# A window-attention and gated-FFN kernel on one core: warm-up matmuls into another bank, full-width maxima, fewer f32 low halves, another order of the work

## The chip, the cores and the metric

One Trainium2 chip, one of its cores. The metric is the device time of one execution in microseconds (us). Besides the timed executions there is one that the hardware profiler took; its page and trace are what "the profile" means below. Engines: PE is TensorE, ACT is ScalarE, DVE is VectorE, POOL is GpSimd; SP only issues DMAs here.

## What is computed

Windowed attention, whose output goes as the activations into a gated feed-forward block:

```python
scores = scale * np.matmul(q, k.transpose(0, 1, 3, 2))      # (8, 8, 576, 576), head size 64
mask = (rel >= 0) & (rel < 64)                              # 64 keys back, causal
attn = softmax(np.where(mask, scores, -1e9))
x = matmul(attn, v).transpose(0, 2, 1, 3).reshape(4608, 512)
h = x @ w_in                                                # 512 -> 2048
sp = np.maximum(h, 0.0) + np.log1p(np.exp(-np.abs(h)))      # softplus
out = (h * erf(sp)) @ w_out                                 # 2048 -> 512
```

The two weight matrices reach the chip as 64-bit floats and are turned into numbers that PE can multiply on the chip itself.

## The kernel before, in words

**Precision.** Every operand of a large product is split into a high and a low half in f16, after scaling by a power of two; a product is the sum of three: high with high, high with low, low with high. The power of two comes from a maximum: of a chunk of q, k and v (`chunk_max`, `chunk_rows`, `chunk_top`, `chunk_all`, `chunk_scale`, L345 to L364), and of a pair of weight pieces (`bound`, `pair_rows`, `pair_top`, `pair_all`, `pair_scale`, L485 to L507). In both, DVE or ACT reduces along the free axis, a small matmul against the identity (L350; L495) lays the 128 partitions' values out in a row, DVE takes the maximum of the row, a second small matmul with a matrix of ones (L358; L501) spreads it over all partitions, and DVE reads it back (L361 into `cpw`; L304 into `kw`).

**Tiles.** 4608 tokens are 36 units of 128 and 18 chunks of 256. A unit's attention is 48 score matmuls of a 64x64 corner of the array (`scores`, L391), masked maximum, subtraction, two exponentials, transposes by DMA, and two times 24 matmuls of 128x64 weights (`weigh`, L424) into the PSUM tile `av`. The feed-forward block runs in 36 groups, a group being one chunk with one half of the 2048 hidden columns. A group is four blocks of 24 matmuls of 256 columns (`mm1`, L569) into one of the two banks `hp`; an eviction of each block by ACT or DVE (`hidden`, L312 or L314); softplus and erf on ACT (L581, L585), each with its own function table, whose loads show as ACT_TABLE_LOAD; a product on DVE (L589); a split into `gh` and `gl` (L312 or L314; L319); and twice 16 matmuls with `gh` and 8 with `gl` of 512 columns (`mm2`, L605) into the two banks `o`.

**Weights.** w_in and w_out come in 16 pieces of 1 MB (`fetch`). A piece is made into f32 by three passes of DVE and ACT (L475, L479, L483), bounded (L489 or L491), and scaled into its high half (`high`). Its low half is made in one of two ways. `low` is one DVE pass (L319). `low_sum` and `low_out` go by PE: an f32 matmul with a diagonal matrix (two passes, L532) and an f16 matmul that subtracts the high half (L533) into an `o` bank, twice for a piece, each followed by an eviction on ACT or DVE (L439 or L441). Before the change 11 pieces go by PE and 5 by DVE. Pieces 0 to 3 are needed before the first group, 4 to 7 before the second, 8 to 11 before the first `mm2`.

**Warm-ups.** `warm` issues matmuls of the identity with itself (L622) whose result nobody reads, at eight places between the start and the first `mm1`, 508 in all. They write `idle`, a stretch of the PSUM tile `av`; the small matmuls for the maxima write other stretches of the same tile (`crow`, `call`, `wrow`, `wall`).

**Order.** All of this is emitted from one list of tokens, `PLAN`, in a manual schedule: each engine runs its instructions in the list's order. A token names a handler, its indices and sometimes an engine (`a` ACT, `v` DVE, `g` POOL). In this text `wm:2:17` is 17 warm-ups, `pb` and `py` the two small matmuls of a chunk's maxima, `mb` and `my` those of a weight pair, `lp` one of a piece's two sums on PE, `s` and `a` a unit's scores and half of its weighing, `mm`, `mA` and `mB` the blocks of `mm1` and the `gh` and `gl` parts of `mm2`, `ev` an eviction of `hp`, `fo` an eviction of `o`. So the order on each engine, and the engine of each step that has a choice, are set by hand in the list.

```python
row_at = HP * (D + 1)
crow, call = avb[:3, 0, row_at:row_at + P], avb[:, 0, row_at + P:row_at + P + 3]
wrow, wall = avb[:1, 1, row_at:row_at + P], avb[:, 1, row_at + P:row_at + P + 1]
idle = avb[:, 0, row_at + P + 3:row_at + P + 123]
```

Of the kernel before, what the change touches and what calls it, by code (L numbers as in the profile page):

```python
# [213 lines left out]
def window_attention_gated_ffn(ctx, tc, q, k, v, w_in, w_out, masks, out):  # L214
# [27 lines left out]
    kwo = fixed("kwo", [P, 2])  # L242
    pm = fixed("pm", [P, 2])
    pr = fixed("pr", [P, 2])
    cmx, cpw, csc, cde = (cells(n, NCH, 3) for n in ("cmx", "cpw", "csc", "cde"))
    ctop, cdiag = fixed("ctop", [3, NCH]), fixed("cdiag", [3, NCH, 3], BF16)
    wtop = fixed("wtop", [1, 8], BF16)
    ident = fixed("ident", [P, P], BF16)
# [442 lines left out]
```

## Time and profile before

| | |
|---|---|
| median of 3 runs | 942.07 us (941.08 to 944.35) |
| the profiled execution | 943.69 us |
| its span, first to last instruction | 941.8 us |
| mean granted clock of PE | 0.982 |
| busy: PE, ACT, DVE, POOL | 906.7, 724.5, 701.2, 238.1 us |
| matmuls | 9282 |

A matmul's busy time includes the way through the array, which overlaps with the next one's; what a block of matmuls costs PE is read from its start to the start of what follows. PE runs its matmuls in the list's order, so such differences add up to the span without gaps or overlaps. Three stretches are told apart below: from the start to the first `mm1` block at 83.3 us, from there to the first `mm2` block of the second group at 185.2 us, by when the last weights have been made, and the rest.

### The profile page before, as it was taken

How to read it: one execution, taken by the hardware profiler on the slowest of the kernel's cores; microseconds unless marked ns; L12 is line 12 of the kernel's file. 1: busy time of each engine (PE TensorE's matmuls, PEld its weight loads, DVE VectorE, ACT ScalarE, POOL GpSimd, SP SyncE). 2: the span in 40 equal slices, each digit the busy share in tenths (PEclk: the TensorE clock that was granted, in tenths of full speed). 3: DMA queues.
4: the chain of work that ended last, by engine and by line, in shares of the span. 5: the costliest groups of instructions: out<-in, count | busy, mean ns of one | idle time of the engine just before them, and what ended most of it. 6: DMA issues, size and time to landing. Idle time of an engine off the chain costs nothing.

```text
span 941.8 us, 22242 instructions
## 1 busy us (share of the span) xinstructions
PE 906.7 (96%) x9282; PEld 606.3 (64%) x9282; DVE 701.2 (74%) x1533; ACT 724.5 (77%) x831; POOL 238.1 (25%) x231
## 2 busy tenths in 40 slices
PE   7778899999999999999999999999999999999998
PEld 6555657756656766666666766666767566676663
DVE  5567788888886877697887778888887776855542
ACT  5657899799974898889869798886969584966452
POOL 0022333320211122022232225341534260501000
PEclk8789899999999999999999999999999999999999
DMA  9655575542342445144543435444433424121000
GB/s 368 243 99 159 93 208 114 151 106 86 95 120 69 115 75 147 30 140 94 121 112 80 113 90 111 126 86 101 107 113 76 117 42 95 33 59 24 23 24 22
DMA packets 140533, 98.63 MB, mean 105 GB/s; under 512 B 117777, under 2 KB 117905, under 8 KB 140433
## 3 DMA queue, kind: packets, MB, share of 16 engines
q1 hardware_dynamic: 140432, 97.22, 40.7%
q8 instruction: 72, 1.18, 0.5%
q14 instruction: 29, 0.23, 0.1%
HBM read 59.44 MB, written 9.44 MB: 73 GB/s over the span
## 4 chain that ended last, share of the span: by engine, by line
PE 80%; ACT 7%; DVE 5%; DMA 5%; issue 1%; POOL 0%; SPq 0%; DVEq 0%; ACTq 0%
PE o L605 34%; PE hp L569 34%; PE av L424 3%; PE o L532 3%; PE av L622 3%; PE s L391 2%; DMA xt<-xs 2%; DMA vr<-v_in 1%; ACT y L581 1%; DMA stage<-w_out 1%; ACT L581 1%; ACT y L585 1%; ACT L585 1%; PE o L533 1%; DVE y L589 1%
## 5 line engine op out<-in xcount | busy, mean ns | idle before, releaser
L569 PE MATMUL hp<-xt,w 128*128 128x256 f16 x3456 | 397.3, 273 | 5.7 <-DMA xt<-xs 5.3
L569 PEld LDWEIGHTS <-w 128*128 128x128 f16 x3456 | 334.6, 98 | 63.8 <-issue 6.0
L605 PE MATMUL o<-w,gh 128*128 128x512 f16 x1152 | 260.7, 380 | 0.6 <-DVE ob L614 0.6
L605 PEld LDWEIGHTS <-gh 128*128 128x128 f16 x1152 | 110.4, 98 | 123.7 <-issue 1.4
L605 PE MATMUL o<-w,gl 128*128 128x512 f16 x576 | 136.5, 380 | 0.0
L405 POOL TENSOR_TENSOR sm<-sm,mx 128x512 f32<-128x512 f32 x56 | 69.4, 1244 | 204.0 <-DVE mx L400 203.9
L581 ACT ACTIVATE y<-h 128x1024 f32<-128x1024 f32 x72 | 75.8, 1056 | 53.4 <-DVE h L314 52.8
L589 DVE TENSOR_TENSOR y<-h,y 128x1024 f32<-128x1024 f32 x72 | 92.2, 1281 | 29.9 <-ACT y L585 29.7
L319 DVE SCALAR_TENSOR_TENSOR gl<-y,sg,gh 128x1024 f16<-128x1024 f32 x72 | 97.5, 1355 | 16.8 <-PE o L605 12.8
L314 DVE TENSOR_SCALAR h<-hp,c 128x512 f32<-128x512 f32 x95 | 70.8, 746 | 42.0 <-PE hp L569 41.4
L581 ACT ACT_TABLE_LOAD x68 | 87.2, 1283 | 7.9 <-DVE h L314 6.7
L605 PEld LDWEIGHTS <-gl 128*128 128x128 f16 x576 | 53.4, 98 | 55.3
L585 ACT ACT_TABLE_LOAD x67 | 86.0, 1283 | 1.2
L585 ACT ACTIVATE y<-y 128x1024 f32<-128x1024 f32 x72 | 75.9, 1056 | 0.8
L400 DVE CUSTOM_DVE_ANT_0 sm<-s,mask 128x128 f32<-128x128 f32 x288 | 65.1, 285 | 11.1 <-PE s L391 10.3
L414 POOL TENSOR_TENSOR p<-sm,p 128x512 f16<-128x512 f32 x36 | 47.8, 1329 | 93.1 <-ACT sm L410 93.0
L409 ACT ACTIVATE p<-sm,shift,cde 128x512 f16<-128x512 f32 x72 | 58.1, 807 | 15.4 <-POOL sm L405 12.1
L447 POOL TENSOR_TENSOR xs<-x,xs 128x512 f16<-128x512 f32 x26 | 36.3, 1397 | 96.9 <-ACT xs L439 59.4
L410 ACT ACTIVATE sm<-sm,shift,cde 128x512 f32<-128x512 f32 x72 | 58.6, 814 | 2.4
L319 DVE SCALAR_TENSOR_TENSOR vs<-vr,csc,vs 128x1024 f16<-128x1024 f32 x36 | 55.0, 1527 | 1.8 <-POOL vs L316 1.5
L312 ACT ACTIVATE gh<-y,sg 128x1024 f16<-128x1024 f32 x39 | 44.3, 1137 | 9.7 <-PE o L605 7.0
L312 ACT ACTIVATE h<-hp,c 128x512 f32<-128x512 f32 x49 | 33.1, 678 | 24.1 <-PE hp L569 24.1
(129 smaller groups left out, 980.3 us busy)
## 6 DMA issues: line engine op xcount, KB each, us to landing
vr<-v_in SPq DMA_DIRECT2D x36, 512.0 KB, 4.1
kr<-k_in SPq DMA_DIRECT2D x36, 384.0 KB, 3.6
qr<-q_in SPq DMA_DIRECT2D x36, 256.0 KB, 3.6
out<-ob SPq DMA_DIRECT2D x36, 256.0 KB, 2.1
stage<-w_out SPq DMA_DIRECT2D x6, 1024.0 KB, 5.0
stage<-w_in SPq DMA_DIRECT2D x4, 1024.0 KB, 7.0
w<-w_in SPq DMA_DIRECT2D x2, 1024.0 KB, 11.0
w<-w_out SPq DMA_DIRECT2D x2, 1024.0 KB, 4.9
```

What stands on the lines that cost most here:

```text
L312: nc.scalar.activation(dst, src, AF.Copy, scale=s)
L314: nc.vector.tensor_scalar(dst, src, s, None, op0=ALU.mult)
L319: nc.vector.scalar_tensor_tensor(dst, src, s, hi, op0=ALU.mult, op1=ALU.subtract)
L400: nc.vector.tensor_tensor_reduce(smi(u, par)[:, j, :], sps[par][:, j, :], mask[:, var, :], 1.0, LOWEST, op0=ALU.add, op1=ALU.max, accum_ou ...
L405: eng_of(eng).tensor_tensor(s, s, m.unsqueeze(2).broadcast_to([P, HP, P]), op=ALU.subtract)
L409: nc.scalar.activation(pp[0][u % 2][:, HP * par:HP * par + HP, :], s, AF.Exp, bias=shift14, scale=es)
L410: nc.scalar.activation(s, s, AF.Exp, bias=shift14, scale=es)
L569: nc.tensor.matmul(hps[pc % 2][:, f, :], w1[a][:, cc, fs], xt[b][c % 2][:, cc, :], start=(n == 0), stop=(n == 3 * NCC - 1))
L581: nc.scalar.activation(at(yb, g, n), at(hb, g, n), AF.Softplus)
L585: nc.scalar.activation(y, y, AF.Erf)
L589: nc.vector.tensor_tensor(y, at(hb, g, n), y, op=ALU.mult)
L605: nc.tensor.matmul(ops[j], a[:, f, ts], w2[b][:, hf * GF + f, :], start=f == 0 and a is gh and b == 0, stop=f == GF - 1 and a is gl)
```

## The change

Four things.

1. `idle` becomes a stretch of the bank `hp0`, and there are 334 warm-ups at seven places in place of 508 at eight.
2. The two small matmuls of a chunk's maxima are given the array's full size. The stationary operand of the first is 128x128 in place of 128x3 (`cmx` is one tile of 128 columns, of which three are used and the others are zero); that of the second is 128x128 ones in place of 3x128, with a moving operand of 128 partitions whose rows from the fourth on are zero. POOL gets two more memsets at the start. The small matmuls of the weight pairs stay as they are.
3. 7 pieces have their low halves made by PE, and 9 by DVE (`lp` and `le` 22 to 14 each, `l` 5 to 9). Of the `lp` tokens that are left out, one stood before the first `mm1` and seven stood between it and the second group's `mm2`; there two are left of nine.
4. `PLAN` is another list. What it computes is the same, and the engines of many steps differ: `ev` is on ACT 88 times and on DVE 56 times (49 and 95 before). A unit's two `a` tokens stand side by side more often, and next to an `s`: PE goes to such attention work and away from it 48 times in place of 86, and changes between `s` and `a` within one such visit 26 times in place of 7. ACT's list has 175 table loads in place of 171.

```diff
-    "L:1 L:0 lq:0 L:3 L:2 lk:0 L:5 lk:1 lq:1 lm wm:0:126 lv:1 lv:0 d:1 c:1 L:4 o:1 b:1:v c:0 d:0 pk:0:0:a o:0 b:0:a "
...
-    cmx, cpw, csc, cde = (cells(n, NCH, 3) for n in ("cmx", "cpw", "csc", "cde"))
-    ctop, cdiag = fixed("ctop", [3, NCH]), fixed("cdiag", [3, NCH, 3], BF16)
+    cpw, csc, cde = (cells(n, NCH, 3) for n in ("cpw", "csc", "cde"))
+    cmx = fixed("cmx", [P, P])
+    ctop, cdiag = fixed("ctop", [3, NCH]), fixed("cdiag", [P, NCH, 3], BF16)
...
-    ones = fixed("ones", [3, P], BF16)
+    ones = fixed("ones", [P, P], BF16)
...
-    crow, call = avb[:3, 0, row_at:row_at + P], avb[:, 0, row_at + P:row_at + P + 3]
+    crow, call = avb[:, 0, row_at:row_at + P], avb[:, 0, row_at + P:row_at + P + 3]
...
-    idle = avb[:, 0, row_at + P + 3:row_at + P + 123]
...
+    idle = hps[0][:, 0, :120]
...
+    nc.gpsimd.memset(cmx, 0.0)
+    nc.gpsimd.memset(cdiag, 0.0)
...
     def chunk_max(c):
-        nc.vector.tensor_reduce(cmx[c], peaks[:, :, c * TPC:(c + 1) * TPC + 1], axis=AX.X, op=ALU.max)
-        exponent(cmx[c], cmx[c])
+        top = cmx[:, :3]
+        nc.vector.tensor_reduce(top, peaks[:, :, c * TPC:(c + 1) * TPC + 1], axis=AX.X, op=ALU.max)
+        exponent(top, top)
 
     def chunk_rows(c):
-        nc.tensor.matmul(crow, powers(cmx[c]), ident, start=True, stop=True)
+        nc.tensor.matmul(crow, powers(cmx), ident, start=True, stop=True)
 
     def chunk_top(c):
         top = ctop[:, c:c + 1]
-        nc.vector.tensor_reduce(top, crow, axis=AX.X, op=ALU.max)
-        nc.vector.scalar_tensor_tensor(cdiag[:, c], top.broadcast_to([3, 3]), FLOOR, ident[:3, :3], op0=ALU.max, op1=ALU.mult)
+        nc.vector.tensor_reduce(top, crow[:3], axis=AX.X, op=ALU.max)
+        nc.vector.scalar_tensor_tensor(cdiag[:3, c], top.broadcast_to([3, 3]), FLOOR, ident[:3, :3], op0=ALU.max, op1=ALU.mult)
```

The lines of the changed kernel stand two higher than those of the kernel before in most of the code (L624 for L622).

**First place: PE in the start-up, at the second weight pair's `my`.** `wtop` is the pair's maximum, `ident` the warm-ups' operand, `diag` and `minus` the operands of a low half. Before:

```order
L533 MATMUL o_155<-w_0_137,minus 128x512
L501 LDWEIGHTS ones
L501 MATMUL av<-wtop,ones 128x1
L622 LDWEIGHTS ident
L622 MATMUL av<-ident 128x120
```

Now:

```order
L535 MATMUL o_156<-w_0_137,minus 128x512
L503 LDWEIGHTS ones
L503 MATMUL av<-wtop,ones 128x1
L352 LDWEIGHTS cmx
L352 MATMUL av<-ident,cmx 128x128
L360 LDWEIGHTS ones
L360 MATMUL av<-cdiag,ones 128x3
L534 MATMUL o_156<-w_0_139,diag_88 128x512
```

Where 52 warm-ups followed (`wm:3:52`), the two matmuls of the first chunk's maxima follow now, ahead of the third piece's sums; they stood behind the warm-ups and behind one of these sums each.

**Second place: PE in the steady part, at the end of unit 18's first `a` token.** `pt` and `vs` are operands of `a`, `qs` and `ks` of `s`. Before, the array goes from the 64-column weights of `a` back to `mm1`; the unit's second `a` token follows a block later:

```order
L424 LDWEIGHTS pt_0_124
L424 MATMUL av<-vs_0_115,pt_0_124 64x65
L424 LDWEIGHTS pt_0_126
L424 MATMUL av<-vs_0_113,pt_0_126 64x65
L569 LDWEIGHTS w_0_137
L569 MATMUL hp_154<-xt_0_133,w_0_137 128x256
```

Now the second `a` token follows at once, and at its end unit 20's scores follow:

```order
L426 LDWEIGHTS pt_0_124
L426 MATMUL av<-vs_0_115,pt_0_124 64x65
L426 LDWEIGHTS pt_0_126
L426 MATMUL av<-vs_0_113,pt_0_126 64x65
L393 LDWEIGHTS qs_0_105
L393 MATMUL s_150<-ks_0_109,qs_0_105 64x128
```

Two `a` tokens and an `s` make one visit, where they made three.

**Third place: ACT between the softplus of groups 13 and 14.** `h<-hp` is an eviction (`ev`), `y<-h` softplus, `y<-y` erf, `p` and `sm` exponentials of the attention, `gh` a high half. Before:

```order
L312 ACTIVATE gh<-y_144,sg 128x1024
L312 ACTIVATE h_141<-hp_153,c_89 128x512
L409 ACTIVATE p_1_121<-sm_118,shift_64,cde 128x512
L410 ACTIVATE sm_118<-sm_118,shift_64,cde 128x512
L312 ACTIVATE h_141<-hp_154,c_89 128x512
L581 ACT_TABLE_LOAD
L581 ACTIVATE y_143<-h_141 128x1024
```

Now:

```order
L583 ACT_TABLE_LOAD
L583 ACTIVATE y_144<-h_142 128x1024
L313 ACTIVATE h_141<-hp_154,c_89 128x512
L587 ACT_TABLE_LOAD
L587 ACTIVATE y_144<-y_144 128x1024
L313 ACTIVATE h_141<-hp_153,c_89 128x512
L583 ACT_TABLE_LOAD
L583 ACTIVATE y_143<-h_141 128x1024
```

Group 14's evictions of `hp` by ACT stand between the passes of softplus and erf and their table loads, where those before stood among the exponentials.

323 rows, old and new, of the table PLAN are left out of this document.

## The prediction

> **What bounds the kernel now.** I read the page's engine line and clock line first, then a table of three stretches (start to the first block of `mm1`; from there until the last weights are made; the rest), then the waits.
>
> ```profile
> PE 906.7 (96%) x9282; PEld 606.3 (64%) x9282; DVE 701.2 (74%) x1533; ACT 724.5 (77%) x831; POOL 238.1 (25%) x231
> PEclk8789899999999999999999999999999999999999
> ```
>
> ```profile
> 0.00:83.30 83.30, 63.65 (x759) 45.23 (x760) 49.33 (x118) 49.08 (x73) 10.66 (x25) 0.84 0.62 206
> 83.30:185.20 101.90, 94.67 (x1104) 69.08 (x1103) 85.29 (x220) 89.44 (x122) 37.61 (x33) 0.97 0.64 161
> 185.20:938.00 752.80, 748.35 (x7422) 491.95 (x7420) 565.87 (x1197) 586.01 (x638) 189.85 (x173) 1.00 0.36 86
> ```
>
> The columns of the table are the stretch, its length, busy time of PE, weight loads, DVE, ACT and POOL, then the granted clock. The third stretch belongs to PE: 748 of 753 us, with ACT at 78% and DVE at 75%. Only less work on PE shortens it. The second is crowded everywhere: PE 93%, ACT 88%, DVE 84%. In the first, PE is busy mostly with warm-ups and low halves, and DVE and ACT are busy for 49 us of 83 each: nothing is full, so a chain of waits sets its length.
>
> **Term 1, warm-ups in another bank: the first stretch.** Where DVE reads the maxima out of `av`, the groups name what it waited for:
>
> ```profile
> L304 DVE TENSOR_SCALAR kw<-av 128x1 int32<-128x1 int32 x8 | 1.3, 159 | 15.5 <-PE av L622 12.5 <-PE av L501 1.7 <-PE av L424 1.3
> L361 DVE COPY cpw<-av 128x3 f32<-128x3 f32 x18 | 2.8, 157 | 19.7 <-PE av L358 8.8 <-PE av L424 5.6 <-PE av L622 5.4
> L498 DVE TENSOR_REDUCE wtop<-av 1x1 bf16<-1x128 f32 x8 | 2.2, 281 | 11.6 <-PE av L495 7.3 <-PE av L622 2.9 <-PE av L424 1.4
> ```
>
> L622 are the warm-ups: 12.5 + 5.4 + 2.9 = 20.8 us of DVE's waits are for matmuls that nobody reads. The timeline of PE and, below it, of DVE shows how:
>
> ```profile
> 24.65 2.95 PE L622 MATMUL av<-ident 128*128 128x120 bf16 x52
> 33.96 3.96 PE L622 MATMUL av<-ident 128*128 128x120 bf16 x71
> 49.08 7.00 PE L622 MATMUL av<-ident 128*128 128x120 bf16 x128
> 64.71 1.54 PE L424 MATMUL av<-vs,pt 128*64 128x65 f16 x48
> 83.33 2.78 PE L569 MATMUL hp<-xt,w 128*128 128x256 f16 x24
> ```
>
> ```profile
> 37.96 0.16 DVE L361 COPY cpw<-av 128x3 f32<-128x3 f32 x1 [5.37 <-PE av L622]
> 56.12 0.16 DVE L304 TENSOR_SCALAR kw<-av 128x1 int32<-128x1 int32 x1 [5.15 <-PE av L622]
> ```
>
> The first chunk's scale is read at 37.96, as the 71 warm-ups end (33.96 + 3.96), though its matmul stands ahead of them. The third pair's scale is read at 56.12, as the 128 end, and the masked maxima of the second unit stand behind it in DVE's queue. Each of these waits holds the first attention, whose weighing starts at 64.71; behind that come the transposes and `mm1`. With `idle` in `hp0`, which no eviction reads before the first groups, the waits go. The new list also puts the first chunk's two matmuls ahead of warm-ups and sums.
>
> The waits follow one another on one queue, so 20.8 us is the ceiling of what their going gives. Late next: the first scores wait for four DVE passes on weight pieces that the new list puts between the scale and them. Such a pass is about as long as a low half's, 1.27 us in a row below; some of it fills time in which DVE would wait for ACT's halves, and I take 3 us in all. That leaves 18; if half of the waits only turn into waits for PE's low-half sums or for weights, 11. With the new order in its favour, 22. Term 1: **-18** (-11 to -22), the first `mm1` at about 65 us. The two new memsets on POOL stand ahead of the first warm-up only, at a time when PE waits for the first weights anyway: nothing.
>
> **Term 2, fewer f32 low halves: the second stretch.** Two consecutive sums, and the passes on DVE and ACT that are exchanged:
>
> ```profile
> 118.11 1.06 PE L532 MATMUL o<-stage,diag 128*128 128x512 f32 x2
> 119.01 0.38 PE L533 MATMUL o<-w,minus 128*128 128x512 f16 x1
> 119.31 0.22 PE L350 MATMUL av<-ident,cmx 128*3 128x128 bf16 x1
> ```
>
> ```profile
> L319 DVE SCALAR_TENSOR_TENSOR w<-stage,sw,w 128x1024 f16<-128x1024 f32 x3 | 3.7, 1274 | 0.0
> L439 ACT ACTIVATE w<-o 128x512 f16<-128x512 f32 x17 | 9.9, 588 | 6.6 <-PE o L533 6.6
> ```
>
> A sum costs PE 119.31 - 118.11 = 1.2 us. Seven fewer in this stretch are 8.4 us of PE (the eighth was before `mm1`, inside term 1). In exchange DVE has four passes of 1.27 us more, 5.1 us in all, and ACT eight evictions of 0.59 us less, 4.7. But PE is not alone here. Of ACT's 89.4 us about 1 us net goes, DVE's 85.3 grows by some 4 to 89. At the most, those two could be busy 97% of a stretch, 92 us; at today's 88% it stays 101. I take 94 us: **-8** (0 to -14, the lower end if waits for weights and transposes go as well).
>
> **Term 3, fewer changes of the array's shape: the third stretch.** PE from the second group's `mm2` on, start by start:
>
> ```profile
> 188.66 1.89 PE L605 MATMUL o<-w,gl 128*128 128x512 f16 x8
> 190.48 0.58 PE L424 MATMUL av<-vs,pt 128*64 128x65 f16 x24
> 190.99 3.63 PE L605 MATMUL o<-w,gh 128*128 128x512 f16 x16
> ...
> 199.42 3.62 PE L605 MATMUL o<-w,gh 128*128 128x512 f16 x16
> 202.96 0.22 PE L350 MATMUL av<-ident,cmx 128*3 128x128 bf16 x1
> 203.11 1.90 PE L605 MATMUL o<-w,gl 128*128 128x512 f16 x8
> 204.95 0.17 PE L358 MATMUL av<-cdiag,ones 3*128 3x3 bf16 x1
> 205.05 3.63 PE L605 MATMUL o<-w,gh 128*128 128x512 f16 x16
> 208.61 0.96 PE L424 MATMUL av<-vs,pt 128*64 128x65 f16 x48
> 209.50 1.90 PE L605 MATMUL o<-w,gl 128*128 128x512 f16 x8
> 211.24 2.02 PE L569 MATMUL hp<-xt,w 128*128 128x256 f16 x17
> ```
>
> Eight `gl` matmuls take 1.74 us ahead of other full-array work (209.50 to 211.24), 1.82 ahead of an `a` (188.66 to 190.48), 1.84 ahead of the ones matmul (203.11 to 204.95): about 0.1 us per change of shape. Leaving an `a` costs the same: alone it takes 0.51 us (190.48 to 190.99), two together 0.89 (208.61 to 209.50), not 1.02.
>
> A chunk's maxima cost PE 0.15 + 0.10 us themselves and 0.2 in the blocks ahead of them, 0.45 us. At full size they need no change of shape and cost what a warm-up does, 7.00 us / 128 = 0.055 each: 0.11. That is 0.34 us less, 14 of the 18 chunks in this stretch: -4.7. And 38 fewer visits to attention work at 0.2 us, less 19 more changes within a visit at 0.1, give 7.6 - 1.9 = 5.7, of which I put 5 here.
>
> A full-size stationary operand takes longer to load:
>
> ```profile
> L622 PEld LDWEIGHTS <-ident 128*128 128x128 bf16 x508 | 32.1, 109 | 3.0 <-POOL ident masks.py:199 1.8 <-issue 1.0
> L350 PEld LDWEIGHTS <-cmx 128*3 128x3 bf16 x18 | 1.5, 81 | 11.1 <-DVE wm L540 3.9 <-issue 3.2 <-DVE cmx L304 1.3
> ```
>
> By these rows 128 columns load in 109 ns and 3 in 81: 28 ns more, and 0.5 us over 18 chunks if nothing hid them. The Trainium skill (TensorE: Matmul & The Clock Gate, section LDWEIGHTS) speaks against the change more strongly: loading time is the number of columns over 1.2 GHz, 2.5 ns against 107, and the sum would lose 1.9 us. The rows don't show a load that shrinks with the columns, so I stay with them.
>
> What stands against these gains of 9.7 us are new waits on DVE and ACT, which get no less work here while PE arrives at every step sooner. Their steps last:
>
> ```profile
> L581 ACT ACT_TABLE_LOAD x68 | 87.2, 1283 | 7.9 <-DVE h L314 6.7
> L581 ACT ACTIVATE y<-h 128x1024 f32<-128x1024 f32 x72 | 75.8, 1056 | 53.4 <-DVE h L314 52.8
> L314 DVE TENSOR_SCALAR h<-hp,c 128x512 f32<-128x512 f32 x95 | 70.8, 746 | 42.0 <-PE hp L569 41.4
> L312 ACT ACTIVATE h<-hp,c 128x512 f32<-128x512 f32 x49 | 33.1, 678 | 24.1 <-PE hp L569 24.1
> ```
>
> One such wait can be read from the list. At the end an `o` bank is evicted by ACT behind group 35's softplus, and the last group's `mm2` needs the bank: an eviction of `hp`, a softplus and this eviction are 0.75 + 1.06 + 0.68 = 2.5 us, beside 1.74 us of `gl` matmuls: 0.8 us lost. I set 3 us for all of them. Term 3: **-6** (-10 if there are none; +8 if PE waits another 14 us).
>
> **The sum.** -18 - 8 - 6 = -32. The profiled execution took 943.69 us, 1.9 beyond its span and 1.6 above the median of 942.07. 943.7 - 32 = 911.7; against the median, 910.
>
> **The rivals.**
>
> *ACT becomes the bound of the third stretch (slower).* 39 evictions of `hp` move from DVE to ACT, some now between softplus, erf and their table loads. ACT gets 39 x 0.68 = 26 us. There are two `hp` banks; an eviction that finds a load and a pass ahead of it comes 1.28 + 1.06 = 2.3 us late, and PE, a block further, waits. It decides from 32 / 39 = 0.8 us of PE's time per moved eviction on; at 1.06, one pass, the price is 41 us and the time 910 + 41 = 951. Against it stand the list of waits
>
> ```profile
> PE hp L569 <- ACT h L312: 0.3, 1, 0.3
> ```
>
> by which PE waited for one of ACT's 49 evictions now, for 0.3 us, and that 586 + 26 us are 81% of the stretch.
>
> *The second stretch takes the gain back.* ACT and DVE, not PE, say when the last weights are ready. If they run at no better a share than now, the second stretch keeps its length (101, -1), and an earlier start finds weights later: -11, -1 and -4 give 942 - 16 = 926. For it: 88% and 84%. Against: in the first stretch the same engines have room.
>
> *The clock falls.* 0.84 in the first stretch means half clock in a third of it ((1 - 0.84) / 0.5). With 174 fewer warm-ups it might be half throughout: the 12 sums ahead of `mm1` at 2.4 in place of 1.2 us are 14 us, of which a third is paid already, and the first products lose a little more: +11, and 921. The Trainium skill (TensorE: Matmul & The Clock Gate, Part 1: The HAM clock gate) has the rule: the gated clock is the default, some 3.4 us of sustained matmuls lift it, an idle window of that length brings it back; it speaks against thinning the warm-ups. The clock line's 8, 7, 8, 9, 8 ahead of the steady 9s agrees that 508 don't hold it either.
>
> *The change doesn't do what it says.* DVE's reads still wait for PE's later work, now the sums or the weighing (L424 holds `cpw` for 5.6 us already). Then term 1 is about -2: 942 - 16 = 926.
>
> **How the numbers follow.** Forecast 0.70; the clock 0.09; the gain taken back 0.11; not what it says 0.04; ACT the bound 0.06. The sums of the bounds are -46 and -3; that all three fall to one end is unlikely, so the range reaches from -44 to the rivals at 921 and 926 with a little over: 898 to 928. A run can tell 0.3%, about 2.8 us, from no change. Every case but one is over that on the fast side; of ACT's 0.06 I give 0.01 to its point of balance: faster 0.94, same 0.01, slower 0.05.
>
> **What would show it.** Term 1: no wait of `kw`, `cpw` or `wtop` on warm-ups, the first `mm1` near 65 us. Term 2: `mA` of the second group near 159 us, with 28 passes at the f32 sums' line in place of 44. Term 3: the chunk's two small matmuls start to start near 0.06 us, a third stretch near 747 us. Wrong: waits of `hp` on ACT's evictions of more than some us, a first stretch above 75 us, or a second one of 100.

## The result, and the profile after

The changed kernel takes 906.70 us (median of 4 runs, 904.16 to 909.69) where the kernel before takes 942.47 (4 runs, 941.08 to 944.35): a ratio of 0.962, 95% interval 0.9585 to 0.9656. Its profiled execution took 905.67 us. The engine and clock lines of its page:

```profile
PE 869.9 (96%) x9084; PEld 593.3 (66%) x9084; DVE 692.9 (77%) x1553; ACT 742.5 (82%) x852; POOL 203.5 (23%) x194
PEclk9989999999999999999999999999999999999999
```

The table of the three stretches, with the columns of the prediction's (length, busy PE, weight loads, DVE, ACT, POOL, clock):

```profile
0.00:59.45 59.45, 46.18 (x582) 32.35 (x582) 48.00 (x116) 47.39 (x71) 14.29 (x28) 0.91 0.84 285
59.45:153.95 94.50, 85.91 (x1083) 66.51 (x1083) 86.35 (x223) 87.33 (x118) 28.26 (x27) 0.96 0.66 175
153.95:899.80 745.85, 737.79 (x7422) 494.41 (x7419) 557.82 (x1215) 607.81 (x665) 160.97 (x140) 1.00 0.37 87
```

The stretches went from 83.3, 101.9 and 752.8 us to 59.5, 94.5 and 745.9: -23.9, -7.4, -6.9. These lengths are of one profiled execution each, and their sum of 38 us stands beside 35.8 us between the medians. In the first, DVE and ACT do what they did (48 and 47 us of work in place of 49 and 49), in 24 us less: waits went, not work.

The groups that waited for the warm-ups, now:

```profile
L305 DVE TENSOR_SCALAR kw<-av 128x1 int32<-128x1 int32 x8 | 1.2, 149 | 0.5 <-PE av L503 0.5
L363 DVE COPY cpw<-av 128x3 f32<-128x3 f32 x18 | 2.8, 155 | 3.0 <-PE av L360 3.0
L500 DVE TENSOR_REDUCE wtop<-av 1x1 bf16<-1x128 f32 x8 | 2.2, 276 | 1.9 <-PE av L497 1.9
```

No row names the warm-ups (L624 here) as what DVE waited for, and the waits that are left are each for the matmul that the instruction reads. PE's timeline in the start-up shows that the warm-ups also stand elsewhere:

```profile
23.82 0.16 PE L360 MATMUL av<-cdiag,ones 128*128 128x3 bf16 x1 [0.74 <-DVE cdiag L357]
24.07 2.08 PE L534 MATMUL o<-w,diag 128*128 128x512 f32 x2
...
27.98 3.52 PE L624 MATMUL hp<-ident 128*128 128x120 bf16 x64
31.43 0.99 PE L393 MATMUL s<-ks,qs 64*64 64x128 f16 x48
...
34.83 1.07 PE L624 MATMUL hp<-ident 128*128 128x120 bf16 x17
35.82 0.97 PE L393 MATMUL s<-ks,qs 64*64 64x128 f16 x48
36.72 5.37 PE L624 MATMUL hp<-ident 128*128 128x120 bf16 x99
```

Behind the chunk's second maxima matmul (23.82) come low-half sums, not warm-ups, and the two long batches, 64 and 99, stand behind a sum and behind scores, whose results lie outside `av`. Behind a weight pair's `my` there are 17 to 19. In the list before, batches of 52, 71 and 128 stood directly behind `my`, `py` and `my`. This matters below.

What is late next stands at the first `mm1`, of which one matmul runs and the others wait for transposes (`xt`):

```profile
59.45 0.28 PE L571 MATMUL hp<-xt,w 128*128 128x256 f16 x1 [1.56 <-DMA xt<-xs]
64.21 6.00 PE L571 MATMUL hp<-xt,w 128*128 128x256 f16 x35 [4.47 <-DMA xt<-xs]
```

So the first block ends only at 68.74 us; before, it ran from 83.33 to 86.04 without a wait. Counted to its end, the first two stretches give -17.3 and -14.0.

In the third stretch, a chunk's maxima on PE's timeline, start by start:

```profile
282.65 0.22 PE L352 MATMUL av<-ident,cmx 128*128 128x128 bf16 x1
282.71 1.89 PE L607 MATMUL o<-w,gl 128*128 128x512 f16 x8
284.43 0.17 PE L360 MATMUL av<-cdiag,ones 128*128 128x3 bf16 x1
284.46 3.61 PE L607 MATMUL o<-w,gh 128*128 128x512 f16 x16
```

0.06 and 0.03 us, and the eight `gl` matmuls between them take 1.72 (282.71 to 284.43) where they took 1.84.

### The profile page after: what moved, and what is told of

It is laid out like the page before. It is cut to its first block, busy times and chain, and to the rows that moved or that the text cites. A ratio compares the mean times of both kernels' runs of the same rounds, so it can differ in the third digit from the quotient of the medians.

```text
span 903.7 us, 21845 instructions
## 1 busy us (share of the span) xinstructions
PE 869.9 (96%) x9084; PEld 593.3 (66%) x9084; DVE 692.9 (77%) x1553; ACT 742.5 (82%) x852; POOL 203.5 (23%) x194
## 4 chain that ended last, share of the span: by engine, by line
PE 72%; ACT 10%; DVE 8%; DMA 5%; issue 3%; POOL 1%; SPq 0%; POOLq 0%; ACTq 0%; DVEq 0%
PE o L607 34%; PE hp L571 32%; PE av L426 3%; PE s L393 2%; DMA pt<-p 1%; DMA xt<-xs 1%; ACT y L583 1%; ACT L583 1%; ACT gh L313 1%; DVE sm L402 1%; ACT sm L412 1%; ACT h L313 1%; PE o L534 1%; ACT p L411 1%; DVE gl L320 1%
## 5 line engine op out<-in xcount | busy, mean ns | idle before, releaser
L591 DVE TENSOR_TENSOR y<-h,y 128x1024 f32<-128x1024 f32 x72 | 90.0, 1253 | 75.3 <-ACT y L587 74.9
L407 POOL TENSOR_TENSOR sm<-sm,mx 128x512 f32<-128x512 f32 x45 | 55.2, 1234 | 200.7 <-DVE mx L402 168.3
L313 ACT ACTIVATE h<-hp,c 128x512 f32<-128x512 f32 x88 | 59.3, 677 | 44.2 <-PE hp L571 35.3
L416 POOL TENSOR_TENSOR p<-sm,p 128x512 f16<-128x512 f32 x42 | 56.5, 1346 | 108.3 <-ACT sm L412 104.1
L315 DVE TENSOR_SCALAR h<-hp,c 128x512 f32<-128x512 f32 x56 | 41.7, 745 | 38.2 <-PE hp L571 34.6
L313 ACT ACTIVATE gh<-y,sg 128x1024 f16<-128x1024 f32 x41 | 46.7, 1140 | 15.1 <-DVE y L591 8.2
L320 DVE SCALAR_TENSOR_TENSOR vs<-vr,csc,vs 128x1024 f16<-128x1024 f32 x36 | 50.7, 1410 | 1.2 <-ACT vs L313 1.2
L449 POOL TENSOR_TENSOR xs<-x,xs 128x512 f16<-128x512 f32 x18 | 27.2, 1509 | 95.0 <-DVE xs L443 77.4
```

Source lines behind the costliest of these rows:

```text
L313: nc.scalar.activation(dst, src, AF.Copy, scale=s)
L320: nc.vector.scalar_tensor_tensor(dst, src, s, hi, op0=ALU.mult, op1=ALU.subtract)
L407: eng_of(eng).tensor_tensor(s, s, m.unsqueeze(2).broadcast_to([P, HP, P]), op=ALU.subtract)
L416: eng_of(eng).tensor_tensor(pp[1][u % 2][:, sl, :], smi(u, par), pp[0][u % 2][:, sl, :], op=ALU.subtract)
L591: nc.vector.tensor_tensor(y, at(hb, g, n), y, op=ALU.mult)
```

## The experiments

Each kernel starts from the one before or the one after the change. The last column has the three stretches as above; the second ends with the first `mm2` of the second group. The kernel before ran again beside the others, with medians of 941.5 to 942.9 us, and each ratio is to the runs beside it.

The lengths are each from one profiled execution, which lies up to 5.4 us from its kernel's median, and a stretch that an edit doesn't touch can differ too: the third stretch, with one and the same list, has 752.8 us before, 753.1 with the warm-ups in `hp0` and 756.1 with four low halves on DVE. So 3 us in one length are not yet an effect.

| kernel | median us | ratio to before (95%) | stretches |
|---|---|---|---|
| before | 942.5 | 1 | 83.3, 101.9, 752.8 |
| before, warm-ups in `hp0` | 921.6 | 0.9793 (0.9750 to 0.9836) | 62.7, 101.8, 753.1 |
| before, four pieces' low halves on DVE | 945.6 | 1.0042 (1.0016 to 1.0067) | 82.1, 102.9, 756.1 |
| before, full-size maxima | 938.2 | 0.9962 (0.9932 to 0.9991) | 85.4, 103.3, 746.5 |
| before, `a` tokens joined | 938.0 | 0.9964 (0.9943 to 0.9984) | 81.1, 100.3, 750.1 |
| before, the first three of these | 920.2 | 0.9763 (0.9730 to 0.9795) | 59.5, 106.4, 751.1 |
| the new list alone | 916.6 | 0.9723 (0.9702 to 0.9745) | 63.7, 99.2, 749.2 |
| after, warm-ups in `av` again | 909.1 | 0.9645 (0.9617 to 0.9674) | 60.4, 94.6, 747.9 |
| after, four pieces back on PE | 913.1 | 0.9704 (0.9664 to 0.9743) | 61.4, 101.7, 749.2 |
| after, no warm-ups | 910.3 | 0.9662 (0.9633 to 0.9690) | 60.7, 98.0, 746.8 |
| after | 906.7 | 0.9620 (0.9585 to 0.9656) | 59.5, 94.5, 745.9 |
| after, two places of the list moved | 904.5 | 0.9590 (0.9568 to 0.9612) | 60.3, 92.5, 745.6 |
| after, two places moved, second unit's halves on DVE | 905.6 | 0.9606 (0.9582 to 0.9630) | 60.8, 94.4, 743.3 |
| after, two places moved, one more piece on DVE | 904.1 | 0.9586 (0.9567 to 0.9605) | 59.0, 97.3, 743.6 |

**Warm-ups in the other bank, nothing else.**

```diff
-    idle = avb[:, 0, row_at + P + 3:row_at + P + 123]
+    idle = hps[0][:, 0, :120]
```

> The kernel before with one line changed: the warm-ups write hp0; list, warm-up counts and all else as before. Theory (the waits of DVE on warm-ups hold the first attention): none of kw, cpw or wtop waits on warm-ups any more, the first weighing starts some 10 us before 64.7, the first mm1 block near 73 us, and the time falls by 8 to 12 us. Rival (the list's order makes the gain, not the bank): the 508 warm-ups still stand on PE ahead of the matmuls that the chain needs, so PE itself becomes late where DVE was; the time falls by less than 4 us.

-20 us, more than either expected. The first stretch is now

```profile
0.00:62.66 62.66, 54.64 (x760) 40.35 (x761) 48.48 (x118) 48.01 (x72) 10.71 (x25) 0.95 0.86 273
```

The first `mm1` comes at 62.66 in place of 83.33: 20.7 us, where DVE's waits on warm-ups were 20.8, with 508 warm-ups, all sums and the old order in place. DVE's idle time in the stretch falls from 34.0 to 14.2 us, so other waits did not take their place: the waits followed one another in full. The other two stretches are what they were. The granted clock rose as well, from 0.84 to 0.95, with the same number of warm-ups. What that gave by itself this run doesn't separate; DVE's waits account for the gain without it.

**Four pieces' low halves by DVE, nothing else** (pieces 7, 10, 11 and 12, the pass where the piece's first sum stood).

```diff
-  lp:7:0 ... lp:7:1 ... le:7:0:v ... le:7:1:v        (pieces 10, 11, 12 alike)
+  l:7
```

> The kernel before with pieces 7, 10, 11 and 12 made by one DVE pass each at the place of their first sum on PE; their sums and evictions are left out, all else as before. Theory (PE pays for each sum on the path): 8 sums of 1.2 us, some at half clock, are 10 us of PE, of which most comes back: 7 to 10 us faster. Rival (DVE and ACT bound the second stretch): DVE gets 5 us more, the second stretch keeps its length, and the time falls by less than 3 us.

Slower, by 0.2 to 0.7%: the theory fell. The rival's mechanism held, the second stretch keeps its length, but not its direction. PE did have its work taken off, the second stretch

```profile
82.07:185.02 102.95, 87.92 (x1083) 67.39 (x1082) 88.80 (x222) 87.91 (x118) 39.48 (x33) 0.93 0.59 160
```

has 87.92 us of it in place of 94.67. But the stretch is 1 us longer. PE's timeline and DVE's show where the 6.8 us went:

```profile
116.01 0.22 PE L350 MATMUL av<-ident,cmx 128*3 128x128 bf16 x1
119.18 0.16 PE L358 MATMUL av<-cdiag,ones 3*128 3x3 bf16 x1 [2.95 <-DVE cdiag L355]
122.77 1.54 PE L424 MATMUL av<-vs,pt 128*64 128x65 f16 x48 [3.44 <-DVE cpw L361]
```

```profile
116.12 1.28 DVE L319 SCALAR_TENSOR_TENSOR w<-stage,sw,w 128x1024 f16<-128x1024 f32 x1
117.31 1.12 DVE L558 TENSOR_SCALAR sg<-rw,csc,isw 128x2 f32<-128x2 f32 x1
118.35 0.26 DVE L559 TENSOR_SCALAR sg<-kwo,cde,wm 128x1 f32<-128x1 f32 x1
118.53 0.21 DVE L553 TENSOR_SCALAR c<-kw,cpw 128x2 f32<-128x2 f32 x1
118.66 0.27 DVE L354 TENSOR_REDUCE ctop<-av 3x1 f32<-3x128 f32 x1
118.97 0.15 DVE L355 SCALAR_TENSOR_TENSOR cdiag<-ctop,ident 3x3 bf16<-3x3 f32 x1
119.05 1.21 DVE L589 TENSOR_TENSOR y<-h,y 128x1024 f32<-128x1024 f32 x1
120.18 1.27 DVE L319 SCALAR_TENSOR_TENSOR w<-stage,sw,w 128x1024 f16<-128x1024 f32 x1
```

Two passes of 1.27 and 1.28 us (116.12 and 120.18) stand in DVE's queue ahead of reads of 0.14 to 0.27 us, `ctop` and `cpw`, for which PE waits; DVE itself has no gap there. The sums that would have filled PE's time are the very ones that were taken out. The list of waits has these two rows, and the kernel before the third:

```profile
PE av L358 <- DVE cdiag L355: 6.5, 3, 3.1
PE av L424 <- DVE cpw L361: 3.7, 2, 3.4
PE av L358 <- DVE cdiag L355: 1.3, 2, 0.8
```

For `cpw` the kernel before waits 0.3 us. The granted clock is lower as well, 0.93 in the stretch where it was 0.97. ACT still makes two diagonals, 0.39 us each, that nobody reads any more.

That explains why nothing was gained, not the loss of 4 us. In the profile the second stretch ends 0.2 us earlier than before (185.0 for 185.2), and the third is 3.3 us longer with the same list: near 375 us PE waits 2.0 us for `xt`, and the granted clock is 0.84 over the 11 us there, 3.8 us lost in all; near 735 us it waits 1.9 us longer for `cmx`; elsewhere it waits less. Whether the edit makes these waits is not shown.

**Full-size maxima, nothing else** (the lines on `cmx`, `cdiag`, `ones` and `crow`, with the old list).

```diff
-    ctop, cdiag = fixed("ctop", [3, NCH]), fixed("cdiag", [3, NCH, 3], BF16)
+    cmx = fixed("cmx", [P, P])
+    ctop, cdiag = fixed("ctop", [3, NCH]), fixed("cdiag", [P, NCH, 3], BF16)
...
-    ones = fixed("ones", [3, P], BF16)
+    ones = fixed("ones", [P, P], BF16)
```

> The kernel before with the chunk maxima's two matmuls at full array size and nothing else. Theory (about 0.1 us per change of the array's shape): 0.34 us for each of 18 chunks, 14 of them where PE is the bound: 4 to 6 us faster, and the two matmuls 0.06 us start to start. Rival (a load of 128 columns costs in proportion to its columns, and the wider operands are loaded in the open): the gain is eaten to 3 us or less.

-0.09 to -0.68%, some 3.6 us. In the profile the third stretch is 6.3 us shorter than before (746.5 to 752.8). Compared start by start, 4.4 us of that lie at the 14 chunks' maxima and the blocks ahead of them, 0.07 to 0.12 us at most of these 56 steps: what the theory said. The other 1.9 us net are PE's waits at other places, such as 1.6 us near 555 us, which went in the run with the low halves on DVE as well, where the maxima are as before. The first two stretches are 2.1 and 1.4 us longer; why is not shown.

**`a` tokens joined, nothing else**: a unit's first `a` token goes down to the second, 86 visits become 69.

```diff
-  a:14:1 gl:12:0 sp:12:1 mA:11:1 er:12:1 gt:12:1 a:14:0 mB:11:1
+  gl:12:0 sp:12:1 mA:11:1 er:12:1 gt:12:1 a:14:1 a:14:0 mB:11:1
```

> The kernel before with the first weighing token of each unit moved down beside the second, so that PE goes to attention work 69 times in place of 86; nothing else. Theory (a visit costs PE 0.2 us in changes of shape): 17 x 0.2 = 3.4 us less work on PE, 2 to 4 us faster. Rival (such changes hide behind other waits, and a late first half delays the unit's normalisation): no difference, or slower by 1 to 3 us.

-3.5 us by the medians, as expected. In its profile the third stretch, where 15 of the 17 visits went, is 2.7 us shorter. The first two are 2.2 and 1.6 us shorter with only two visits fewer, so that part of its profile has other reasons.

**The first three together, in the old list.**

> The kernel before with the bank of the warm-ups, the full-size maxima and the four pieces by DVE together, in the old list (508 warm-ups). If the three parts add up as they did alone (-20, -3.5, +4 us): about 922 us, and the new list is worth the remaining 15 us. If the low halves by DVE pay only once the start-up is short: about 912 us, and the list is worth 5.

920.2: the parts add up (942.5 - 20 + 4 - 3.6 = 923, 0.3% above what was measured). Some 13.5 us more come only with the new list.

**The four pieces back on PE, in the new list.**

```diff
-  l:7
+  lp:7:0 le:7:0:a lp:7:1 le:7:1:a                   (pieces 10, 11, 12 alike, with their diagonals)
```

> The changed kernel with pieces 7, 10, 11 and 12 given back to PE (22 sums), each evicted by ACT, placed where the DVE pass stood or, for piece 10, behind its high half. If the low halves by DVE are worth nothing in any list, as they were in the old one: the same time within 3 us or faster. If they pay in this list, which was made for them: 5 to 11 us slower, in the second stretch.

+6.4 us by the medians, and the second stretch

```profile
61.41:163.13 101.72, 91.78 (x1102) 68.61 (x1100) 81.04 (x217) 89.96 (x126) 27.52 (x27) 0.98 0.60 158
```

is 7.2 us longer, with 5.9 us more of PE. (This profiled execution took 918.5 us, 5.4 above the median; the new list alone, below, has the same order and 99.2 us there, 4.7 longer.) The edit that gained nothing in the old list is worth 6 us here. DVE's passes stand at other places in the new list, and the wait of PE on `cdiag` is 0.7 us in the whole kernel after:

```profile
L360 PE MATMUL av<-cdiag,ones 128*128 128x3 bf16 x18 | 3.0, 168 | 0.7 <-DVE cdiag L357 0.7
```

That the places make the difference is argued from these waits, not shown by a run that moves the passes alone; and each list was made for its own choice of engine.

**The warm-ups back in `av`, in the new list.**

```diff
-    idle = hps[0][:, 0, :120]
+    idle = avb[:, 0, row_at + P + 3:row_at + P + 123]
```

> The changed kernel with the warm-ups writing the tile av again. 334 warm-ups stand in the list, most of them behind a matmul whose result DVE reads. Theory (DVE's reads wait for them): 6 to 12 us of DVE waits on warm-ups come back, most of it behind the 99 ahead of the first weighing, and the time rises by as much. Rival (the new list places the reads so that the bank does not matter): within 3 us.

Within the interval of the kernel after: the rival was right. In DVE's list of waits the only row left that names warm-ups is

```profile
DVE kw L307 <- PE av L626: 2.3, 2, 1.4
```

2.3 us, where it was 20.8. The order shown above does it: what stands directly behind a maxima matmul is short or writes another bank.

**The new list alone**: the code before, with the new list and the four pieces on PE.

> The new list alone: the code of the kernel before (warm-ups into the bank that av uses, maxima on 3 rows) and the list of the kernel after, with pieces 7, 10, 11 and 12 put back on PE. The runs from the kernel after showed +2 us for the warm-ups put back into the av bank and +6.4 us for the four pieces put back on PE, and the run of the full-size maxima alone showed -3.6 us. Theory, that most of the gain is the list's and that the three other edits add up on top of it: 906.7 + 2.3 + 6.4 + 3.6 = 919 us, ratio about 0.975 (0.971 to 0.979), the first matmul of the FFN at 60 to 64 us although the warm-ups stand in the av bank. Rival, that the list needs the edits it was made with (without the idle bank and the DVE's sums it only shifts the waits): 927 us or more, ratio 0.984 or more, with DVE waits on the warm-ups of several us as before.

916.6 us, a little under the theory's 919. The first `mm1` comes at 63.7 us with all warm-ups in `av`; DVE waits for warm-ups for

```profile
DVE kw L305 <- PE av L623: 3.2, 2, 2.3
```

So the list alone makes 26 of the 36 us, and the bank alone makes 20 of them in the old list: the two take away the same waits, and each leaves the other little to do.

**No warm-ups at all** (all seven `wm` tokens left out; nobody reads their results).

```diff
-  lq:0 L:3 L:2 wm:0:98 lk:0
+  lq:0 L:3 L:2 lk:0
```

> The changed kernel without any warm-up. If the clock is what they are for: the granted clock of the first stretch falls from 0.89 to about 0.6, the sums ahead of mm1 take 2.1 to 2.4 us each, the first products run at half speed for some us, and the time rises by 6 to 12 us. If waits hide a slow clock in the start-up: within 3 us.

+3.6 us by the medians, with overlapping intervals: between the two, nearer to the rival. The clock does fall. Rows of its table from 20 to 60 us (first two) and of the kernel after's:

```profile
20.00:40.00 20.00, 9.22 (x118) 4.35 (x115) 18.81 (x58) 18.20 (x26) 4.97 (x4) 0.74 0.92 346
40.00:60.00 20.00, 13.34 (x118) 6.44 (x119) 16.51 (x40) 16.14 (x27) 7.15 (x5) 0.67 0.66 144
```

```profile
20.00:40.00 20.00, 17.47 (x280) 12.55 (x279) 18.97 (x58) 18.32 (x28) 4.99 (x4) 0.91 0.96 356
40.00:60.00 20.00, 14.72 (x179) 8.78 (x176) 17.94 (x45) 17.53 (x30) 7.17 (x5) 0.91 0.65 140
```

At 0.67 to 0.74 PE is busy for 9 to 13 of 20 us, while DVE and ACT are busy for 16 to 19: a slow clock of an engine that isn't the bound there costs little. The first `mm1` comes 1.2 us later.

**Two places of the new list moved**: the second unit's normalization, halves and transposes ahead of a weight scale, and the result rows of group 34 both on DVE.

```diff
-  mb:3 mx:3 pa:1 ... h:6:a pb:1 wm:6:18 n:1 dg:3 ... xh:1:a ... xt:1:0 xl:1:g ... xt:1:1
+  mb:3 mx:3 n:1 xh:1:a xt:1:0 xl:1:g xt:1:1 pa:1 ... h:6:a pb:1 wm:6:18 dg:3 ...
-  fo:34:1:v fo:34:0:a mA:35:0
+  fo:34:0:v fo:34:1:v mA:35:0
```

> The kernel after with two moves in its list: result rows of group 34 both on DVE (before the last mA ACT's eviction came 2.12 us late), and the second unit's normalization, high part, low part and transposes put ahead of the third w_in chunk's scale (POOL waited 10.30 us for the high part and PE 4.47 us for the transposes that came of it). Theory, that these two waits are late for their place in the list alone: the wait of PE on the transposes inside the first FFN block falls from 4.5 to about 1.7 us (the low part 2.8 us earlier) and the wait of 2.1 us at the end falls below 0.5: 906.7 - 2.8 - 1.8 = 902 us, ratio 0.957. Rival, that the time of the start-up is set by the sum of ACT's or DMA's work and the wait comes back later in the second stretch: only the end's 1.8 us, 905 us, ratio 0.960.

904.5 us; its interval overlaps that of the kernel after, so the time alone doesn't tell them apart. The trace shows what moved: the first block of `mm1` runs through, and PE's rows behind it are

```profile
60.32 5.40 PE L573 MATMUL hp<-xt,w 128*128 128x256 f16 x48
...
67.23 0.81 PE L395 MATMUL s<-ks,qs 64*64 64x128 f16 x44 [1.28 <-DVE ks L322]
67.97 0.33 PE L499 MATMUL av<-ident,acc 128*1 128x128 bf16 x3
70.22 6.81 PE L573 MATMUL hp<-xt,w 128*128 128x256 f16 x48 [1.93 <-DVE h L317]
```

The first block (24 of the 48 matmuls) ends at 62.94, 5.8 us earlier, but the first `mm2` comes at 95.17 in place of 96.05. In between DVE and ACT are full:

```profile
62.94:95.17 32.23, 27.71 (x378) 21.63 (x376) 30.67 (x80) 31.00 (x42) 11.88 (x11) 0.95 0.73 197
```

95 and 96% busy, and PE waits for DVE, 1.28 us on `ks` and 1.93 on `h`. The rival was right that the wait comes back, though not on ACT or the transfers that it named: nearly 6 us of wait were worth 1. The wait at the end fell from 2.1 to 1.1 us.

**The same with the second unit's halves on DVE.**

```diff
-  xh:1:a xt:1:0 xl:1:g
+  xh:1:v xt:1:0 xl:1:v
```

> The same two moves, with the second unit's high and low part both on DVE instead of ACT and POOL. Theory, places in the list alone: the low part is ready some 3.5 us earlier than in the kernel after, PE's wait on the transposes falls from 4.5 to about 1 us, and ACT, which is 95% busy in the second stretch, is given 0.6 us: 901.5 us, ratio 0.9565. Rival, that DVE's 1.1 us more ahead of the chunk's scales delays the reads on which PE waits: 904 to 906 us, ratio 0.959 to 0.961, with new PE waits on DVE's cdiag or cpw.

905.6: no different. It is the rival's time, but not by the waits on `cdiag` and `cpw` that it named; the new one is on `kw`, 1.4 us.

**One more piece on DVE.**

```diff
-  dg:4 ... lp:8:0 ... lp:8:1 ... le:8:1:v ... le:8:0:a
+  l:8
```

> The list of the run before this one (the kernel after with the second unit's transposes and the end's result rows moved), and piece 8's low half taken off PE as well: one DVE pass of 1.28 us instead of two f32 sums of PE (2 x 1.2 us), one eviction of 0.6 us each on DVE and ACT and ACT's diagonal of 0.4 us. In the kernel after, the four pieces of the change gave 6.4 us together, 1.6 us a piece. Theory, that PE and ACT bound the second stretch of this list and DVE has room: the second stretch falls from 92.5 to about 91 us, 904.5 - 1.6 = 903 us, ratio 0.957. Rival, that DVE is as full as they are by now (95% in the second stretch of that run): the stretch stays at 92.5 or grows by up to 1.5 us with PE waits on DVE's small reads, 904.5 to 906 us, ratio 0.959 to 0.961.

904.1: the same time, so the rival's. PE's work in the first two stretches fell by 1.1 us, yet they took 3.5 us longer, and the third 1.9 less. The rival's reason is not shown: in this run DVE is busy for 88.7 of the second stretch's 97.3 us, 91% and not more than the 95% before. The longest wait of PE there is 3.6 us for `xt`, where the run before it waited 1.2; what delays it is open. This is the lowest median of all, but not by more than its interval.

## Why the prediction was right, and where it wasn't

906.7 us stand against a forecast of 910 and a range of 898 to 928. The signs and the order of the three terms are right: -18, -8 and -6 forecast, -23.9, -7.4 and -6.9 measured. Two of the reasons are not the ones given, and that the sum still came so close is in part luck: the first term is beyond its own range of -11 to -22, and the second does not stand by itself.

**Term 1.** The mechanism was right: the waits on warm-ups are gone, and with the bank alone the first stretch is 20.7 us shorter. The mis-sized step is "late next", 3 us for DVE's passes ahead of the scores: the first scores start at 31.43, as the 64 warm-ups ahead of them end, without a wait. Late next were the second unit's transposes instead, inside the first `mm1` block: 1.56 and 4.47 us. Hence a first `mm1` at 59.5 in place of 65, and -17.3 by the block's end. The step on the cause was incomplete: the new list was put down as a helper of the bank (22 in place of 18), but it takes the same waits away without it. Nor was 20.8 a ceiling for the list, which also brings other steps forward.

On its rule of PSUM the Trainium skill (PSUM — Partial Sum Buffer, section "PSUM bank collisions raise a hardware error") says that semaphores have to guard PSUM by bank and quadrant, or simply by bank, and not by address. The trace before agrees that a read waits for later matmuls at other addresses of its bank, 5.4 us at one place; what such a guard costs is for the list to decide, 20.8 or 2.3 us here.

**Term 2.** The number came out, -7.4 for -8, and a stretch of 94.5 for the 94 that was taken; 28 f32 passes stand at the sums' lines, and PE's work fell from 94.67 to 85.91 us. But the step "seven fewer in this stretch are 8.4 us of PE", bounded by how full DVE and ACT could get, failed as a term of its own: with just that edit the stretch is 1.1 us longer and the kernel no faster. PE's 6.8 us did go, and came back as waits for small reads that stand behind the added passes in DVE's queue. Only in the new list do the same four pieces give 6.4 us. The prediction looked at how busy DVE is, not at what stands behind the added passes in its queue. DVE's load was mis-sized as well, 86.4 us for the 89 foreseen: with the sums, three evictions left DVE in this stretch (and six, not eight, left ACT), and one of the four passes (piece 7) stands ahead of the first `mm1`.

**Term 3.** Right in kind and size. 0.06 + 0.03 us per chunk's maxima were measured for 0.11. In the old list the full-size maxima give 4.4 us at their places in the third stretch, for the 4.7 forecast, and with 15 visits fewer the stretch is 2.7 us shorter, where the forecast put 5 us on 38 fewer visits and 19 more changes within them. The waits set against it, 3 us in all, show as

```profile
PE o L607 <- ACT ob L313: 2.1, 1, 2.1
PE hp L571 <- ACT h L313: 0.9, 1, 0.9
PE o L607 <- DVE ob L616: 0.8, 1, 0.8
```

The one at the end was read from the list at 0.8 us and took 2.1. ACT's rows there:

```profile
886.31 1.28 ACT L583 ACT_TABLE_LOAD   x1 [6.84 <-DVE h L315]
887.60 1.06 ACT L583 ACTIVATE y<-h 128x1024 f32<-128x1024 f32 x1
888.56 0.67 ACT L313 ACTIVATE ob<-o,sg 128x512 f32<-128x512 f32 x1
```

The working counted an eviction, a softplus and an eviction. ACT's table load of 1.28 us stands behind the same wait for the `hp` eviction, and was left out.

On the loads, full-size operands took 98 ns in the kernel after, and nothing of it shows in the starts:

```profile
L352 PEld LDWEIGHTS <-cmx 128*128 128x128 bf16 x18 | 1.8, 98 | 4.6 <-DVE cmx L305 2.6 <-DVE wm L542 0.9
```

The 1.9 us estimated from the Trainium skill's rule of columns over 1.2 GHz (TensorE: Matmul & The Clock Gate, section LDWEIGHTS) are not there, nor is the saving that the rule would give a load of three columns, which took 81 ns before the change.

**The rivals.** ACT as the bound: 88 evictions of `hp`, and PE waited 0.9 us for them. The gain taken back: the second stretch fell to 94.5 and not to 101, in the full change; this rival describes the four pieces alone, and the moved transposes afterwards. The clock: 0.91 in the first stretch in place of 0.84, with 174 warm-ups fewer, and 0.95 with all 508 once the waits were gone, so 0.84 was not what 508 can hold. Even none at all cost 3.6 us by the medians, not 11: the rival took PE for the bound of that stretch. The change not doing what it says: no row names warm-ups.

What stays open: the new list alone shortens the three stretches by 19.6, 2.7 and 3.6 us. The first is for the most part the waits on warm-ups, 3.2 us in place of 20.8; joined `a` tokens gave 2.7 of the third in the old list. Which of its other moves makes the rest was not taken apart. Open is also where the 4 us come from that the four pieces cost in the old list.

## What to carry to other kernels

A wait on work that nobody reads can be removed by another bank or by another order; before the two are added up, try each alone, since they may be the same microseconds. Work that is moved to an engine with room is worth its time on the old engine only if nothing that others wait for stands behind it in the new one's queue: the same four passes gained nothing in one list, which got 4 us slower, and gave 6 us in another. And a long wait at the front of a crowded stretch is worth only what its neighbours can use, here 1 us of 6.

## What was not expected of the hardware

Without any warm-up the granted clock stayed at 0.67 to 0.74 for 40 us, and the whole kernel lost about 3.6 us by the medians, with overlapping intervals. The Trainium skill (TensorE: Matmul & The Clock Gate, Part 1: The HAM clock gate) has the gated clock as the default, and the rows agree; but here the time hardly followed the clock, since DVE and ACT were the busier engines there. A matmul of 3 columns with a full-size operand takes 0.03 us from its start to the next one's in a stream of full-size matmuls, where the same product with an operand of 3 rows took 0.10 and added 0.1 to the block ahead of it.
